# Down projection: more K tiles in seven-product form, one y buffer reloaded in halves, two operand sum buffers

## The chip, the cores and the metric

The kernel runs on one core of one Trainium2 chip. The metric is the device time of one execution in microseconds, given as the median of several runs. The profile is of one execution.

Names of the engines: PE is the tensor engine (PEld its weight loads), DVE the vector engine, ACT the scalar engine, POOL is GpSimd, and SP is the queue that issues the DMAs.

## The reference

One transformer block on x of 2048 tokens by 1024 columns, in bf16: a modulated layer norm, linear attention, a residual, a second modulated layer norm, and a gated feed-forward network with a residual. The part that matters here is the last line of the feed-forward network and its residual:

```python
def _B_ref(x, w_gate, w_up, w_down):              # D = 1024, F = 3584
    return _gelu(x @ w_gate) * (x @ w_up) @ w_down
...
h = _layernorm(x, axis=-1) * (1 + cb) + sb
x = x + gb * _B_ref(h, B_w_gate, B_w_up, B_w_down)
```

The product with `w_down` has 2048 rows, K = 3584 (28 K tiles of 128) and 1024 columns.

## The kernel before

Everything up to the feed-forward network stays as it is. The network runs in 28 units (`unit(u)`): two halves of the tokens, each with 14 units of 256 columns of F. Every unit leaves `y`, the gated product, for two K tiles of the down projection, and `y_store` writes it to a scratch tensor in DRAM (`scr_y`). `x1`, the input of the last residual, is also parked in DRAM (`scr_x`).

The down projection works on the 16 chunks of 128 tokens in eight pairs (ca, cb). A pair with the 1024 output columns in two halves is a 2 by 2 block product, once two K tiles (index r = 0, 1) are taken together: the left side has the blocks a0, a1 (chunk ca) and b0, b1 (chunk cb), the right side four blocks of w_down of 128 by 512. Instead of eight block products the kernel makes seven (Strassen-Winograd) for a number `nj(ca)` of such groups j, and the plain eight for the K tiles that are left (`down`, over `fcs`). The seven products are called P1 to P7. `d_prod(ca, b0, k)` issues Pk as `nj` matmuls of 128x128 by 128x512 into one of the four PSUM banks of the pair (b0 is 0 or 4).

- P1 and P2 take y and w_down as they are, in bf16.
- P5, P6, P7, P3 and P4 take sums of y blocks (`d_s(ca, i)`, i = 0 to 4, here called S0 to S4) and sums of w_down blocks (`d_t(i, q)`), both in the f32r type. S0 = b0 + b1, S1 = S0 - a0, S2 = a0 - b0, S3 = a1 - S1 are made on DVE, S4 is a copy of b1 made on ACT. P5 reads S0, P6 S1, P7 S2, P3 S3 and P4 S4. The sums of the weights are made once, for each part q of w_down (`WDT[q]`), and stay in SBUF.
- Between products, ACT and DVE copy or add PSUM banks (`dpcp`, `ducp`, `descp`, `dpadd`), so that each bank ends up with one quarter of the pair's output.
- `evac` then multiplies a quarter by the gate row (`x2a`), adds x1 (`x2b`) and stores it: two DVE instructions and one DMA.

Before the change `nj` is 6 for the first pair and 11 for the others; the sums have three buffers (`DS`); y of a pair has two alternating buffers `YA` for 22 K tiles and one buffer `YB` for the other 6; x1 comes in whole pairs into two buffers `XD`. The order of the products in a pair is P2 P6 P5 P7 P3 P4, and then the plain matmuls with P1 of the next pair among them (`d_first`). In the last pair plain matmuls are mixed in between, and P3 goes last, into a free bank, with the gate already multiplied into its weights (`t_gb`).

The order on each engine is the order in which these functions emit it; only the part before the second feed-forward unit is reordered by a planner (`sch.reorder`). Every buffer is a fixed stretch of one SBUF arena, and a tracker (`IntervalTracker`) adds the waits that follow from reads and writes of the same bytes or of the same PSUM bank. An engine, and SP too, takes its instructions strictly in order, so a DMA that waits holds up those emitted after it. Each SP DMA also waits for the DMA eight before it.

Of the kernel before, what the change touches and what calls it, by code (L numbers as in the profile page):

```python
# [65 lines left out]
NDJ = 11  # L66
NDJ0 = 6
NJQ = (2, 2, 2, 2, 2, 1)
WDQ = [OFF_R3, OFF_R3 + 8192, OFF_R3 + 16384, OFF_WS, OFF_HT + 16384, OFF_WS + 16384, OFF_WS + 8192, OFF_WS + 20480]
FCQ = [0, 4, 8, 12, 16, 20, 22, 26, NFC]  # L70
OFF_DT = (tuple(OFF_XALL + i * 4096 for i in range(4)), tuple(OFF_XALL + i * 4096 for i in range(4, 8)),
          (OFF_XALL + 32768, OFF_XALL + 36864, OFF_GUH, OFF_GUH + 4096),
          (OFF_TMP + 4096, OFF_TMP + 8192, OFF_R3 + 24576, OFF_YS[0]),
          (OFF_HT + 8192, OFF_HT + 12288, OFF_YS[1], OFF_YS[2]),
          (OFF_GAB, OFF_GAB + 2048, OFF_ROW, OFF_ROW + 2048))
OFF_DS = [OFF_YT + i * 5632 for i in range(3)]
OFF_XD = [OFF_HT + 24576, OFF_HT + 28672]
OFF_YA = [OFF_YT + 45056, OFF_YT + 16896]
OFF_YB = OFF_YT + 28160
# [250 lines left out]
def bass_adaLN_cond__linear_attn_block__geglu_ffn__prompt_kernel(  # L330
# [15 lines left out]
    scr_y = nc.dram_tensor("scr_y", [2 * CPG, P, NFC, 2 * P], bf16).ap()  # L346
    scr_x = nc.dram_tensor("scr_x", [P, NCH, D], bf16).ap()
    scr_rd = nc.dram_tensor("scr_rd", [NSG, 2, HPG, NG, SGW // 2], f32).ap()
    with ExitStack() as es:
# [31 lines left out]
        WDT = [at(f"wd{q}", [P, FCQ[q + 1] - FCQ[q], D], bf16, WDQ[q]) for q in range(8)]  # L381
        DT = [[at(f"dt{q}{i}", [P, NJQ[q], 512], f32r, o_) for i, o_ in enumerate(l)] for q, l in enumerate(OFF_DT)]
        DH = [at(f"dh{q}", [P, NJQ[q], 2, 512], f32r, WDQ[q]) for q in range(6)]
        DS = [at(f"ds{i}", [P, NDJ, P], f32r, OFF_DS[i]) for i in range(3)]
        DS0 = [at(f"dp{i}", [P, NDJ0, P], f32r, OFF_XD[i]) for i in range(2)]
# [962 lines left out]
        def wd_dma(q):  # L1348
            f0, f1 = FCQ[q], FCQ[q + 1]
            sch.dma(Q, lambda e: e.dma_start(WDT[q][:], wd_v[:, f0:f1, :]), wr=[t_ for fc in range(f0, f1) for t_ in r_wd(fc)], note=f"wd{q}")  # L1350
# [196 lines left out]
        def r_xd(c_, c0=0, c1=D):  # L1547
            i = c_ // 2 % 2
            o_ = OFF_XD[i] + c_ % 2 * 2048
            return [(o_ + c0 * 2, o_ + c1 * 2, f"xd{i}")]  # L1550

        def x_in(i):
            sch.dma(Q, lambda e: e.dma_start(XD[i % 2][:], scr_x[:, 2 * i:2 * i + 2, :]), wr=r_xd(2 * i) + r_xd(2 * i + 1), deps=[x_st[i // 2]], note=f"xd{i}")

        def y_in(i):
            sch.dma(Q, lambda e: e.dma_start(YA[i % 2][:], scr_y[i, :, 0:2 * NDJ, :]), wr=[(OFF_YA[i % 2], OFF_YA[i % 2] + NDJ * 1024, f"ya{i % 2}")],
                    deps=[y_st[u] for u in range(i // CPG * NFP, i // CPG * NFP + NDJ)], note=f"ya{i}")

        def yb_in(i):
            sch.dma(Q, lambda e: e.dma_start(YB[:], scr_y[i, :, 2 * NDJ:NFC, :]), wr=[(OFF_YB, OFF_YB + (NFC - 2 * NDJ) * 512, "yb")],  # L1560
                    deps=[y_st[u] for u in range(i // CPG * NFP + NDJ, (i // CPG + 1) * NFP)], note=f"yb{i}")

        def evac(c_, k, b, c0, c1):
            n = c1 - c0
            X_ = XD[c_ // 2 % 2][:, c_ % 2, c0:c1]
            sch.op(V, lambda e: e.tensor_tensor(PS(b, 0, n), PS(b, 0, n), GBB[:, c0:c1], ALU.mult), prd=pr(b), pwr=pr(b), rd=R_GBB, note=f"x2a c{c_}.{k}")
            sch.op(V, lambda e: e.tensor_tensor(X_, PS(b, 0, n), X_, ALU.add), prd=pr(b), rd=r_xd(c_, c0, c1), wr=r_xd(c_, c0, c1), note=f"x2b c{c_}.{k}")
            sch.dma(Q, lambda e: e.dma_start(out_v[:, c_, c0:c1], X_), rd=r_xd(c_, c0, c1), note=f"out{c_}.{k}")

        def r_y(c_, fc):  # L1570
            i, h = c_ // 2, c_ % 2
            o_, name = (OFF_YA[i % 2] + fc * 512, f"ya{i % 2}") if fc < 2 * NDJ else (OFF_YB + (fc - 2 * NDJ) * 512, "yb")
            return [(o_ + h * 256, o_ + h * 256 + 256, name)]

        def y_at(c_, fc):
            i, h = c_ // 2, c_ % 2
            return YA[i % 2][:, fc, h * P:(h + 1) * P] if fc < 2 * NDJ else YB[:, fc - 2 * NDJ, h * P:(h + 1) * P]

        def down(c_, k, b, c0, c1, fcs, last, after):
            n, o = c1 - c0, None  # L1580
            for fc in fcs:
                q, m = wq_of(fc)
                o = sch.op(T, lambda e, fc=fc, q=q, m=m: e.matmul(PS(b, 0, n), y_at(c_, fc), WDT[q][:, m, c0:c1], start=False, stop=last and fc == fcs[-1], skip_group_check=True),  # L1583
                           rd=r_y(c_, fc) + r_wd(fc), pwr=(pr(b) if after and fc == fcs[0] else ()), note=f"down c{c_} k{k} fc{fc}", overwrite_ok=after)
# [13 lines left out]
        def d_t(i, q):  # L1598
            j0, j1 = 0, NJQ[q]
# [11 lines left out]
            sch.op(V, lambda e: e.tensor_tensor(dst, in0, in1, ALU.subtract), rd=r0 + r1, wr=wr, note=f"{'dtsum' if j1 - j0 == 2 else 'dtone'} {q}.{i}")  # L1611

        DSB = (0, 1, 2, 0, 1)

        def nj(ca):
            return NDJ0 if ca == 0 else NDJ

        def ds_ap(ca, i, j0, j1):
            k = DSB[i]
            if ca == 0 and i < 2:  # L1620
                return DS0[k][:, j0:j1, :], [(OFF_XD[k] + j0 * 512, OFF_XD[k] + j1 * 512, f"dp{k}")]
            return DS[k][:, j0:j1, :], [(OFF_DS[k] + j0 * 512, OFF_DS[k] + j1 * 512, f"ds{k}")]

        def y_ap(c_, r, j0, j1):
            i, h = c_ // 2, c_ % 2
            return (YA[i % 2][:, 2 * j0 + r:2 * j1 - 1 + r:2, h * P:(h + 1) * P], [t_ for j in range(j0, j1) for t_ in r_y(c_, 2 * j + r)])

        def d_s(ca, i):
            cb, n = ca + 1, nj(ca)
            for j0, j1 in ((0, min(n, 6)), (6, n)):  # L1630
# [12 lines left out]
        def t_gb(q):  # L1643
            n = NJQ[q]
            t_, r_ = dt_ap(q, 3, 0, n)
            sch.op(V, lambda e: e.tensor_tensor(t_, t_.bitcast(f32), GBB[:, 512:1024].unsqueeze(1).to_broadcast([P, n, 512]), ALU.mult), rd=r_ + R_GBB, wr=r_,
                   note=f"{'dtsum' if n == 2 else 'dtone'} gb{q}")

        def d_prod(ca, b0, k, own=None):
            b = b0 + {1: 0, 2: 0, 5: 3, 6: 2, 7: 2, 4: 2, 3: 1}[k] if own is None else own  # L1650
            i = {1: None, 2: None, 5: 0, 6: 1, 7: 2, 3: 3, 4: 4}[k]
            o, n = None, nj(ca)
            for j in range(n):
# [5 lines left out]
                else:  # L1659
# [3 lines left out]
                    if i == 4:  # L1663
                        dst = dst.rearrange("p (h c) -> p h c", h=2)
                o = sch.op(T, lambda e, l_=l_, r_=r_, j=j, dst=dst: e.matmul(dst, l_[:, 0, :], r_, start=(k in (1, 5) or own is not None) and j == 0, stop=j == n - 1, skip_group_check=True),  # L1665
                           rd=rl + rr, pwr=(pr(b) if j == 0 else ()), note=f"down P{k} c{ca} j{j}", overwrite_ok=True)
# [4 lines left out]
        later = []  # L1671

        def evac_part(c_, k, b, c0, c1):
            X_ = XD[c_ // 2 % 2][:, c_ % 2, c0:c1]
            sch.op(V, lambda e: e.tensor_tensor(DE[:, :], PS(b), GBB[:, c0:c1], ALU.mult), prd=pr(b), rd=R_GBB, wr=R_DE, note=f"x2a c{c_}.{k}")
            sch.op(V, lambda e: e.tensor_tensor(DE[:, :], DE[:, :], X_, ALU.add), rd=r_xd(c_, c0, c1) + R_DE, wr=R_DE, note=f"x2b c{c_}.{k}")

        def evac_sum(c_, k, b, c0, c1):
            X_ = XD[c_ // 2 % 2][:, c_ % 2, c0:c1]
            sch.op(V, lambda e: e.tensor_tensor(X_, PS(b), DE[:, :], ALU.add), prd=pr(b), rd=R_DE, wr=r_xd(c_, c0, c1), note=f"x2b c{c_}.{k}")  # L1680
            sch.dma(Q, lambda e: e.dma_start(out_v[:, c_, c0:c1], X_), rd=r_xd(c_, c0, c1), note=f"out{c_}.{k}")

        def d_first(i):
            b0 = i % 2 * 4
            d_prod(2 * i, b0, 1)
            sch.op(A, lambda e: e.activation(PS(b0 + 2), PS(b0), ACTF.Copy), prd=pr(b0), pwr=pr(b0 + 2), note="dpcp")  # L1686

        def d_pair(i, hook):
# [3 lines left out]
            parts = tuple((ca + n // 2, n % 2, b0 + n, n % 2 * 512, n % 2 * 512 + 512) for n in range(4))  # L1692
            for k in (2, 6, 5, 7, 12, 4, 14, 15, 13, 3) if last else (2, 6, 5, 7, 3, 4):
                if k > 10:
                    x = parts[k - 12]
                    down(*x, fcs, True, True)
                    if k == 13:
                        evac_part(*x)
                    else:
                        evac(*x)  # L1700
                    continue
# [257 lines left out]
```

## Time and profile before

| | |
|---|---|
| median of 3 runs | 786.52 us (786.47 to 786.85) |
| the profiled execution | 786.35 us |
| its span | 784.6 us |
| PE busy | 774.4 us |
| DVE busy | 625.8 us |
| ACT busy | 375.0 us |
| DMA queue time, share of 16 engines | 59.6% |

The span runs from the first to the last instruction of the profiled execution. Matmuls are pipelined: their durations overlap, so a matmul's cost on PE is the spacing of two of them and not the duration in the list. The feed-forward units end at 602.2 us of the span and the down projection fills the rest. In the profile L1442 is a matmul of a feed-forward unit, L1665 one of the seven products, L1583 a plain one; L1641 and L1636 are the sums S0 to S3 and S4, L1566 and L1567 the two instructions of an eviction, L1556 and L1560 the loads of y.

### The profile page before, as it was taken

Reading aid. Unit: us, or ns where it says so; the run is one execution under the profiler, and the core shown is the slowest. Engines: PE = TensorE matmul, PEld = TensorE weight load, DVE = VectorE, ACT = ScalarE, POOL = GpSimd, SP = SyncE. Lnnn points to the kernel's source line nnn. Section 1 sums busy time; section 2 is a strip of 40 time slices with the busy share of each in tenths; the row PEclk is TensorE's granted clock in tenths of the full one; section 3 lists DMA queues with packets and bytes.
Section 4 is the critical chain, followed back from the end, with each engine's and each line's share of the span. In section 5 each row is a group of like instructions: output and inputs, shape, how many; then the busy total and the mean of one; then the engine's idle time right before and its main releaser. Section 6 shows DMA issues by size and latency. Waiting matters only on the chain.

```text
span 784.6 us, 10665 instructions
## 1 busy us (share of the span) xinstructions
PE 774.4 (99%) x3832; PEld 490.2 (62%) x3890; DVE 625.8 (80%) x949; ACT 375.0 (48%) x636; POOL 47.1 (6%) x126
## 2 busy tenths in 40 slices
PE   8999999999999999999999999999999999999998
PEld 4444445666445666767676776767676566666665
DVE  6699998895789878787989889898987975555586
ACT  2497743242565477877755555465654011111011
POOL 2131300000321011100000000000000000000000
PEclk9999999999999999999999999999999999999999
DMA  9789749939998257866344764534327644333411
GB/s 287 250 173 244 163 94 248 221 74 194 203 285 226 82 155 193 242 177 198 108 135 126 242 198 154 159 108 134 113 76 246 239 160 140 124 91 128 159 57 33
DMA packets 178781, 130.24 MB, mean 166 GB/s; under 512 B 69020, under 2 KB 163492, under 8 KB 176680
## 3 DMA queue, kind: packets, MB, share of 16 engines
q1 hardware_dynamic: 178712, 129.55, 59.6%
q8 instruction: 31, 0.51, 0.3%
q14 instruction: 22, 0.18, 0.1%
q10 hardware_dynamic: 16, 0.00, 0.0%
HBM read 92.55 MB, written 23.35 MB: 148 GB/s over the span
## 4 chain that ended last, share of the span: by engine, by line
PE 71%; DVE 1%; issue 0%; DVEq 0%
PE ps_all L1442 44%; PE ps_all L1665 17%; PE ps_all L1583 6%; PE ps_all L1268 4%; DVE h2a L726 0%; DVE xall L1276 0%; DVE xd L1680 0%; DVE ys L1472 0%; DVEq L1914 0%
## 5 line engine op out<-in xcount | busy, mean ns | idle before, releaser
L1442 PE MATMUL ps_all<-ss,tp 128*128 128x512 f32 x896 | 214.3, 396 | 0.0
L1442 PEld LDWEIGHTS ps_all<-ss,tp 128*128 128x128 f32 x896 | 168.2, 188 | 37.8 <-DVE ss L1397 0.3
L1465 ACT ACTIVATE ge<-ps_all 128x512 f32<-128x512 f32 x112 | 64.1, 597 | 74.3 <-DVE ps_all L1453 61.8
L1442 PE MATMUL ps_all<-h2a,wt 128*128 128x512 bf16 x421 | 95.6, 379 | 1.8
L1472 DVE TENSOR_TENSOR ys<-ge,ps_all 128x512 bf16<-128x512 f32 x112 | 74.4, 684 | 5.8 <-PE ps_all L1442 2.9
L1460 DVE TENSOR_TENSOR ps_all<-ps_all,es 128x512 f32<-128x512 f32 x54 | 37.7, 699 | 50.6 <-ACT es L1450 50.3
L1665 PE MATMUL ps_all<-dt,ds 128*128 128x512 f32 x320 | 76.2, 395 | 0.0
L1442 PEld LDWEIGHTS ps_all<-h2a,wt 128*128 128x128 bf16 x448 | 38.0, 98 | 57.2 <-ACT ps_all L1447 16.9
L1417 DVE TENSOR_TENSOR tp<-wt 128x1024 fp32r<-128x1024 bf16 x56 | 68.1, 1216 | 2.1 <-DMA wt<-in_B_w_up_dram 2.1
L1665 PEld LDWEIGHTS ps_all<-dt,ds 128*128 128x128 f32 x320 | 60.1, 188 | 13.4
L1417 DVE TENSOR_TENSOR tp<-wt,tp 128x1024 fp32r<-128x1024 bf16 x56 | 68.2, 1218 | 0.0
L933 PE MATMUL ps_all<-h1T,wq 128*128 128x512 bf16 x256 | 56.7, 379 | 0.0
L882 PE MATMUL ps_all<-wk,h1T 128*128 128x512 bf16 x239 | 55.3, 379 | 1.2 <-DMA wk<-in_A_wqkv_dram 0.5
L1268 PE MATMUL ps_all<-w,pq 128*128 128x512 bf16 x250 | 55.6, 379 | 0.4
L1442 PE MATMUL ps_all<-ar,tp 128*128 128x512 f32 x224 | 55.5, 390 | 0.0
L871 ACT ACTIVATE eb<-ps_all 128x512 f32<-128x512 f32 x64 | 36.4, 593 | 37.6 <-PE ps_all L882 14.8
L1442 PEld LDWEIGHTS ps_all<-ar,tp 128*128 128x128 f32 x224 | 42.0, 188 | 8.9
L1686 ACT ACTIVATE ps_all<-ps_all 128x512 f32<-128x512 f32 x8 | 4.7, 582 | 87.4 <-PE ps_all L1665 87.4
L1447 ACT ACTIVATE ps_all<-ps_all 128x512 f32<-128x512 f32 x56 | 32.6, 582 | 27.1 <-PE ps_all L1442 27.1
L933 PEld LDWEIGHTS ps_all<-h1T,wq 128*128 128x128 bf16 x256 | 24.9, 98 | 30.0
L1268 PEld LDWEIGHTS ps_all<-w,pq 128*128 128x128 bf16 x256 | 24.7, 98 | 30.0 <-ACT w L1200 0.3
L1583 PE MATMUL ps_all<-wd,yb 128*128 128x512 bf16 x185 | 42.6, 379 | 0.5
(148 smaller groups left out, 1016.0 us busy)
## 6 DMA issues: line engine op xcount, KB each, us to landing
wt<-in_B_w_gate_dram SPq DMA_DIRECT2D x28, 512.0 KB, 4.0
wt<-in_B_w_up_dram SPq DMA_DIRECT2D x28, 512.0 KB, 5.3
scr_y<-ys SPq DMA_DIRECT2D x28, 512.0 KB, 2.9
ya<-scr_y SPq DMA_DIRECT2D x8, 1408.0 KB, 6.6
rb<-scr_rd SPq DMA_DIRECT2D x32, 256.0 KB, 6.6
wmst<-in_w_mod_dram SPq DMA_DIRECT2D x6, 1024.0 KB, 5.7
wd<-in_B_w_down_dram SPq DMA_DIRECT2D x6, 1024.0 KB, 7.4
wmq<-in_w_mod_dram SPq DMA_DIRECT2D x8, 512.0 KB, 6.7
```

The source lines that it names most:

```text
L871: sch.op(A, lambda e: e.activation(EB[i][:, :], PS(bank), ACTF.Exp), prd=pr(bank), wr=rng, note=f"{note}.exp")
L882: o = sch.op(T, lambda e, dc=dc: e.matmul(PS(bank), H1[sg][:, ci, dc, :], W_[:, dc, jg * 512:(jg + 1) * 512], start=(dc == 0), stop=(dc == ...
L933: o = sch.op(T, lambda e, dc=dc: e.matmul(PS(b), WQ[:, dc, qc * P:(qc + 1) * P], H1[sg][:, :, dc, :], start=(dc == 0), stop=(dc == NDC - 1 ...
L1268: last[half] = sch.op(T, lambda e, g=g, half=half: e.matmul(PS(b0 + half), PQ[sg][:, g, ci * P:(ci + 1) * P], W2[:, g, half * 512:(half + ...
L1417: sch.op(V, lambda e: e.tensor_tensor(TP[k][:], in0, in1 if k in (0, 2) else in1[:], ALU.subtract), rd=r0 + r1, wr=r_tp(k), deps=[x1_ops[7 ...
L1442: o = sch.op(T, lambda e, l_=l_, r_=r_, dc=dc: e.matmul(PS(b), l_, r_, start=fresh and dc == 0, stop=dc == ND2 - 1, skip_group_check=True) ...
L1447: sch.op(A, lambda e: e.activation(PS(BB + t), PS(BA + t), ACTF.Copy), prd=pr(BA + t), pwr=pr(BB + t), note="pcp")
L1460: sch.op(V, lambda e: e.tensor_tensor(PS(BC + t), PS(BC + t), ES[t][:, :], ALU.add), prd=pr(BC + t), rd=r_2k(OFF_ES[t], f"es{t}"), pwr=pr( ...
L1465: sch.op(A, lambda e: e.activation(GE[i][:, :], PS(b), ACTF.Gelu_apprx_tanh), prd=pr(b), wr=r_2k(OFF_GE[i], f"ge{i}"), note="gelu")
L1472: sch.op(V, lambda e: e.tensor_tensor(YS[s_][:, 2 * h:2 * h + 2, t, :], q(GE[i][:, :]), q(PS(b + 1)), ALU.mult), rd=r_2k(OFF_GE[i], f"ge{i ...
L1583: o = sch.op(T, lambda e, fc=fc, q=q, m=m: e.matmul(PS(b, 0, n), y_at(c_, fc), WDT[q][:, m, c0:c1], start=False, stop=last and fc == fcs[- ...
L1665: o = sch.op(T, lambda e, l_=l_, r_=r_, j=j, dst=dst: e.matmul(dst, l_[:, 0, :], r_, start=(k in (1, 5) or own is not None) and j == 0, st ...
```

## The change

- `nj` becomes 6 for the first pair, 12 for the next two and 14, all 28 K tiles, for the last five.
- w_down is held in seven equal parts of four K tiles, and all seven get their sums. The sums of the last one lie where y of pair 1 was, and are made during pair 2 and the start of pair 3.
- y of a pair lies in two tiles, one for each r, 14 K tiles each. There is one such pair of tiles, `YA[0]`, for all pairs but pair 1, which has its own, `YA[1]`. From pair 2 on, the tile of r = 0 is loaded for the next pair as soon as S2 is made, that of r = 1 as soon as S4 is made (`y_next`). In pair 2, whose plain matmuls still read groups 12 and 13, those two groups are loaded after them (the loads noted `yt`).
- The scratch tensor of y is laid out by r, so that a store's pieces are 512 bytes instead of 1024.
- The operand sums have two buffers, each in two halves of seven groups; a pair uses them in turn.
- x1 comes in quarters (128 tokens by 512 columns) with one buffer each (`XQ`), instead of whole pairs with two.
- The order in a pair is P1 P5 P6 P2 P7 P3 P4, with the plain matmuls of one quarter after P2 and of the other three after P4 (pairs 1 and 2). In the last pair P3 is split: groups 6 to 13 go into its own bank before P4, groups 0 to 5 last.
- The evictions of pair 0 move into pair 1. The load of the fourth part of w_down is issued one unit earlier, and the y of pair 1 ahead of the last part of w_down.

The diff, cut to its core (in `ds_ap`, `k` and `h` are the buffer and its half):

```diff
-NDJ = 11
-NDJ0 = 6
-NJQ = (2, 2, 2, 2, 2, 1)
+NDJ = NFC // 2
+NJP = (6, 12, 12, NDJ, NDJ, NDJ, NDJ, NDJ)
+NSJ = NDJ // 2
...
-    scr_y = nc.dram_tensor("scr_y", [2 * CPG, P, NFC, 2 * P], bf16).ap()
+    scr_y = nc.dram_tensor("scr_y", [4 * CPG, P, NDJ, 2 * P], bf16).ap()
...
-        DS = [at(f"ds{i}", [P, NDJ, P], f32r, OFF_DS[i]) for i in range(3)]
-        XD = [at(f"xd{i}", [P, 2, D], bf16, OFF_XD[i]) for i in range(2)]
+        SB = [[at(f"sb{k}{h}", [P, NSJ, P], f32r, o_) for h, o_ in enumerate(l)] for k, l in enumerate(OFF_SB)]
+        XQ = [at(f"xq{n}", [P, 512], bf16, o_) for n, o_ in enumerate(OFF_XQ)]
...
-        YA = [at(f"ya{i}", [P, 2 * NDJ, 2 * P], bf16, OFF_YA[i]) for i in range(2)]
-        YB = at("yb", [P, NFC - 2 * NDJ, 2 * P], bf16, OFF_YB)
+        YA = [[at(f"ya{i}{r}", [P, NDJ, 2 * P], bf16, o_) for r, o_ in enumerate(l)] for i, l in enumerate(OFF_YA)]
...
+        def y_in(i, r, j0=0, j1=NDJ):
+            a = ya_of(i)
+            sch.dma(Q, lambda e: e.dma_start(YA[a][r][:, j0:j1, :], scr_y[2 * i + r, :, j0:j1, :]), ...)
...
         def ds_ap(ca, i, j0, j1):
-            k = DSB[i]
+            if ca == 0:
+                k, h = ((0, 0), (1, 0), (0, 1), (1, 1), (0, 0))[i]
+            else:
+                k, h = (ca // 2 + i) % 2, j0 // NSJ
...
         def d_pair(i, hook):
             ...
-            for k in (2, 6, 5, 7, 12, 4, 14, 15, 13, 3) if last else (2, 6, 5, 7, 3, 4):
+            def y_next(r):
+                if i > 1 and not last:
+                    y_in(i + 1, r, 0, nj(ca))
+
+            for k in (1, 5, 6, 2, 7, 3, 4):
                 if last and k == 3:
-                    d_prod(ca, b0, 3, 0)
-                    evac_sum(*parts[1][:2], 0, *parts[1][3:])
+                    d_prod(ca, b0, 3, None, range(6, NDJ))
+                    evac_part(*parts[1])
                     continue
                 d_prod(ca, b0, k)
+                if k == 1:
+                    d_cp(b0 + 2, b0, "dpcp")
                 elif k == 5:
+                    d_ecp(b0 + 3)
+                    d_s(ca, 2)
+                elif k == 6:
+                    d_add(b0 + 1, b0 + 2)
+                    d_s(ca, 3)
+                    y_next(0)
+                elif k == 2:
+                    fin(0)
                 elif k == 7:
+                    d_add(b0 + 3, b0 + 2)
+                    d_s(ca, 4)
+                    y_next(1)
+                    if not fcs:
+                        fin(3)
+                elif k == 3:
+                    if not fcs:
+                        fin(1)
+                    d_s(ca + 2, 0, (0, 1) if nj(ca) == nj(ca + 2) else (0,))
+                else:
+                    ns = (3, 1, 2) if fcs else (2,)
+                    for n in ns:
+                        std(n)
+                    if not last and nj(ca) != nj(ca + 2):
+                        for r in range(2):
+                            y_in(i + 1, r, nj(ca), NDJ)
+                    for n in ns[:-1]:
+                        evac(*parts[n])
+                    if not last and nj(ca) != nj(ca + 2):
+                        d_s(ca + 2, 0, (1,))
+                    evac(*parts[ns[-1]])
+                    if last:
+                        d_prod(ca, b0, 3, 0, range(6))
+                        evac_sum(*parts[1][:2], 0, *parts[1][3:])
+                    else:
+                        d_s(ca + 2, 1)
                 hook(k)
...
         DMAS = {...
-                14: lambda: wd_dma(0), 15: lambda: y_in(0), 16: lambda: wd_dma(1), 18: lambda: wd_dma(2)}
+                14: lambda: wd_dma(0), 15: lambda: (y_in(0, 0), y_in(0, 1)), 16: lambda: wd_dma(1), 18: lambda: wd_dma(2), 26: lambda: wd_dma(3)}
...
-        wd_dma(5)
-        wd_dma(7)
-        yb_in(0)
-        y_in(1)
+        y_in(1, 0)
+        y_in(1, 1)
+        wd_dma(6)
...
         def hooks(i):
             def hook(k):
...
+                if i == 1:
+                    if k == 1:
+                        y_in(2, 0)
+                        y_in(2, 1)
+                    if k in (1, 5):
+                        for n in (0, 1) if k == 1 else (2, 3):
+                            evac(*parts_of(0)[n])
+                    if k == 6:
+                        x_in(1, 0, 1, 2, 3)
+                else:
+                    if k == 1:
+                        x_in(i, 0, 3, 1)
+                    elif k == 5:
+                        x_in(i, 2)
+                    if i == 2 and k in (1, 2, 7, 3):
+                        d_t({1: 0, 2: 1, 7: 2, 3: 3}[k], 6)
+                    if i == 3 and k == 1:
+                        d_t(4, 6)
+                    if not more and k in (5, 6):
+                        for q in {5: (0, 1), 6: (2,)}[k]:
+                            t_gb(q)
```

`std(n)` issues the plain matmuls of quarter n, `fin(n)` those and then its `evac`.

More of the change, by code (lines that the diff above doesn't have):

```diff
@@ L511, in wq_of @@
         def wq_of(fc):
-            q = next(q for q in range(8) if fc < FCQ[q + 1])
-            return q, fc - FCQ[q]
+            return divmod(fc, 4)
         def r_wd(fc):
@@ L1559, in yb_in, with r_xq @@
-        def yb_in(i):
-            sch.dma(Q, lambda e: e.dma_start(YB[:], scr_y[i, :, 2 * NDJ:NFC, :]), wr=[(OFF_YB, OFF_YB + (NFC - 2 * NDJ) * 512, "yb")],
-                    deps=[y_st[u] for u in range(i // CPG * NFP + NDJ, (i // CPG + 1) * NFP)], note=f"yb{i}")
-        def evac(c_, k, b, c0, c1):
[L1564 to L1568, printed above, removed]
+        def r_xq(n):
+            return [(OFF_XQ[n], OFF_XQ[n] + 1024, f"xq{n}")]
@@ L1678, in evac_sum @@
         def evac_sum(c_, k, b, c0, c1):
[L1679 to L1686, printed above, removed]
+            n = 2 * (c_ % 2) + k
@@ L1691, in d_pair @@
             fcs = list(range(2 * nj(ca), NFC))
-            parts = tuple((ca + n // 2, n % 2, b0 + n, n % 2 * 512, n % 2 * 512 + 512) for n in range(4))
-            for k in (2, 6, 5, 7, 12, 4, 14, 15, 13, 3) if last else (2, 6, 5, 7, 3, 4):
[L1694 to L1701, printed above, removed]
+            parts = parts_of(i)
@@ L1719, in d_pair @@
-                if last and k in (6, 7):
-                    for q in range(3):
-                        t_gb(q if k == 6 else q + 3)
-                for x in mine:
-                    evac(*x)
-                if 0 < i and not last and k in (7, 3, 4):
-                    d_s(ca + 2, {7: 2, 3: 0, 4: 1}[k])
-                hook(k)
-                if i == 0 and k == 7:
-                    down(*parts[0], list(range(12, 16)), False, True)
-            assert not later
-            if last:
-                return
```

213 lines of the change are left out of this document (106 added, 107 removed).

## The prediction

> **What bounds the kernel now.** I read the page's parts 1, 2 and 4 first: which engine is busy, whether it is busy everywhere, and who is on the chain that ended last.
>
> ```profile
> span 784.6 us, 10665 instructions
> ...
> PE 774.4 (99%) x3832; PEld 490.2 (62%) x3890; DVE 625.8 (80%) x949; ACT 375.0 (48%) x636; POOL 47.1 (6%) x126
> ...
> PE   8999999999999999999999999999999999999998
> ...
> PEclk9999999999999999999999999999999999999999
> ...
> PE 71%; DVE 1%; issue 0%; DVEq 0%
> ```
>
> TensorE (PE) works without a break at the full granted clock, and the chain is made of its matmuls. So the time is the number of matmuls times their spacing, plus whatever makes PE wait. Next come the windows of one FFN unit and one down-projection pair, the chain inside that pair, and the list of waits from 590 us on.
>
> ```profile
> 475.26:487.82 12.56, 12.49 (x56) 8.86 (x56) 10.80 (x14) 6.73 (x13) 0.00 (x0) 1.00 0.67 209
> 641.47:663.93 22.46, 22.39 (x101) 14.75 (x101) 14.59 (x20) 3.12 (x5) 0.00 (x0) 1.00 0.54 186
> ```
>
> ```profile
> 641.47 0.07 issue
> 641.54 3.83 PE ps_all L1583 x17
> 645.37 2.37 PE ps_all L1665 x11
> 647.75 1.29 PE ps_all L1583 x6
> 649.04 14.89 PE ps_all L1665 x66
> 663.93 0.07 issue
> ```
>
> ```profile
> PEld ps_all L1583 <- issue: 2.6, 10, 0.3
> ...
> DVE ds L1641 <- DMA ya<-scr_y: 1.0, 1, 1.0
> ```
>
> A pair today is 101 matmuls in 22.46 us: 46 in bf16 (24 plain, 11 each of P1 and P2) and 55 in f32 (P5, P6, P7, P3, P4). No data holds PE up; its only gap is 0.07 us once per pair, where an f32 run ends and a bf16 run begins. An FFN unit is 16 bf16 and 40 f32 matmuls in 12.56 us. Two equations, 16b + 40f = 12.56 and 46b + 55f = 22.46, give b = 0.2163 us for a bf16 matmul and f = 0.2275 us for an f32 one, each stretch holding one such gap. This is the most important reading: the change swaps the cheap kind for the dear kind.
>
> **The change part by part. Matmuls.** With n groups of two K tiles in products, a pair costs 7n + 4(28 - 2n) = 112 - n matmuls. Pair 0 keeps n = 6. Pairs 1 and 2 go from 11 to 12, pairs 3 to 7 from 11 to 14: 2 + 15 = 17 groups more. One group replaces 8 plain bf16 matmuls by 2 bf16 and 5 f32: 6 x 0.2163 - 5 x 0.2275 = 0.160 us. Seventeen groups give **-2.73 us**. Counted by pair: pairs 1 and 2 become 40b + 60f = 22.30 us, pairs 3 to 7 become 28b + 70f = 21.98 us.
>
> The Trainium skill, page "TensorE: Matmul & The Clock Gate", section "Back-to-back issue gap", puts the isolated gap at N/2.4 + 2.5 ns, about 216 ns for 512 columns, with no difference between types; by it 17 matmuls fewer would be worth 3.7 us. The trace agrees for b and disagrees for f.
>
> **Order.** P1 P5 P6 P2 P7 P3 P4 instead of P2 P6 P5 P7 P3 P4 plain P1 has an f32 run end twice in pairs 1 to 6 (before: once) and once in the last (before: twice): five ends more at the 0.07 us gap shown, **+0.35 us**. Its bounds are 0 and 0.35: no run end is removed on balance, so a gain is excluded.
>
> **Operand sums and evictions.** These are the vector engine's (DVE) and scalar engine's (ACT) pieces:
>
> ```profile
> L1641 DVE TENSOR_TENSOR ds<-ya 128x768 fp32r<-128x768 bf16 x15 | 14.3, 951 | 1.0 <-DMA ya<-scr_y 1.0
> ...
> L1641 DVE TENSOR_TENSOR ds<-ya 128x640 fp32r<-128x640 bf16 x14 | 11.5, 818 | 0.0
> ...
> L1636 ACT ACTIVATE ds<-ya 128x768 fp32r<-128x768 bf16 x8 | 6.7, 839 | 0.0
> ...
> L1636 ACT ACTIVATE ds<-ya 128x640 fp32r<-128x640 bf16 x7 | 5.1, 728 | 0.0
> ```
>
> ```profile
> 659.59 3.29 DVE L1641 TENSOR_TENSOR ds<-ya 128x768 fp32r<-128x768 bf16 x4
> ...
> 666.69 0.69 DVE L1566 TENSOR_TENSOR ps_all<-ps_all,gbb 128x512 f32<-128x512 f32 x1
> 667.41 0.69 DVE L1567 TENSOR_TENSOR xd<-ps_all,xd 128x512 bf16<-128x512 f32 x1
> 668.02 0.69 DVE L1566 TENSOR_TENSOR ps_all<-ps_all,gbb 128x512 f32<-128x512 f32 x1
> ```
>
> A half of seven groups (896 elements) takes 951 + 133 = 1084 ns on DVE and 839 + 111 = 950 ns on ACT. Back to back the halves overlap a little (four took 3.29 us, not 3.54), so I space them by 1.0 us. One eviction (two instructions) is 1.33 us. DVE then has per pair 8 x 1.08 + 4 x 1.33 + 2 x 0.7 = 15.4 us in 22: not the bound. What counts is the order, since with two sum buffers each sum waits for the product that read its buffer: S2 for P5, S3 for P6, S4 for P7, the next S0 for P3, the next S1 for P4.
>
> **Reload of y.** The y buffer is single now, so the second half for the next pair is issued on SP only after S4 has read it. These are the transfers near in size, and the same load in the crowded stretch from 603 us:
>
> ```profile
> ya<-scr_y SPq DMA_DIRECT2D x7, 1408.0 KB, 6.6
> ...
> out_dram<-xd SPq DMA_DIRECT2D x32, 128.0 KB, 2.2
> yb<-scr_y SPq DMA_DIRECT2D x8, 384.0 KB, 3.5
> ```
>
> ```profile
> ya<-scr_y SPq DMA_DIRECT2D x1, 1408.0 KB, 10.1
> ```
>
> A line through 384 and 1408 KB gives 3.03 us per 1024 KB: 5.05 us for a half of 896 KB, 4.64 for 768 KB, 2.7 for 128 KB. Readers of a finished product start about 0.26 us after PE goes on: 0.17 us because a matmul lasts 395 ns at 228 spacing, and 0.09 us as at the end of the chain:
>
> ```profile
> L1665 PE MATMUL ps_all<-dt,ds 128*128 128x512 f32 x320 | 76.2, 395 | 0.0
> ```
>
> ```profile
> 779.00 2.52 PE ps_all L1665 x11
> 781.52 0.03 issue
> ...
> 781.61 0.69 DVE xd L1680
> ```
>
> Steady pair (3 to 7), from its first matmul: P1 ends at 3.03, P5 6.21, P6 9.40, P2 12.43, P7 15.61, P3 18.80, P4 22.05 us. S4's second half runs 15.87 to 16.82; SP issues the reload at 16.9; it lands at 21.95. S0 of the next pair is done in halves at 23.05 and 24.05, and P5 wants it at 25.08. DVE then evicts one quarter (25.4) and makes S1's first half (26.5); P6 wants it at 28.26. With 0.25 us for a weight load not yet in flight, 1.5 us are left. So the reload may take up to 6.6 us, which is just what the larger 1408 KB took: bounds 3.5 to 6.6, no stall at either end, **0**. Queued behind it on SP are only output stores and the x1 quarters, wanted 12 us later. The first half is issued after S2 (about 7.6 us) and lands by 13.
>
> Pair 2 to pair 3 differs: the plain matmuls at its end read groups 12 and 13, so these come as two 128 KB loads only when pair 2's last plain matmuls are done. From pair 2's start: P7 ends 14.25, the main second half is issued at 15.3 and lands at 19.95, S0's first half is done at 21.05, two evictions run to 23.6, plain ends at 22.30, the small loads are issued at 22.4 and 22.75. Pair 3's P1 wants group 12 at 24.97. With the 2.2 us of the 128 KB store they land at 24.6 and 24.95; S0's second half ends 26.1, an eviction comes before S1 on DVE, S1's first half ends 28.45, P6 wanted it at 28.58 less 0.25: stall 0.1. With 2.7 us from the line: 0.4 in P1, 0.2 in P6, together 0.6. With the 3.5 us of 384 KB: 1.4. Below, 0. I take **+0.4 us**, between the row of the same size and the line; S1 late again in pair 3 is absorbed by the 1.5 us.
>
> The skill's page "DMA: Bandwidth & Descriptors", section "Anatomy of one DMA", fits 2.0 us plus bytes at 436 GB/s, an estimate of 2.3 us for 128 KB, with which the stall would be about 0.2; its 5.3 us for 1408 KB is below the 6.6 measured.
>
> **Edits at nothing.** The stores of y go out in pieces of 512 instead of 1024 bytes. These rows bound them:
>
> ```profile
> wt<-in_B_w_gate_dram SPq DMA_DIRECT2D x28, 512.0 KB, 4.0
> ...
> scr_y<-ys SPq DMA_DIRECT2D x28, 512.0 KB, 2.9
> ```
>
> If a store takes the weights' 4.0 instead of 2.9 us, the three ys buffers and 12.56 us per unit hide it; without them it would cost 1.1 us a unit. One w_down load goes a unit earlier on SP; it waits for that unit's P2, and only a store a unit later stands behind it. In pair 0 the y of pair 1 is issued ahead of the last part of w_down; S0 of pair 1, which once waited 1.0 us for its y, has it earlier, and that part is wanted 17 us later. Pair 0's evictions and the last w_down sums move into DVE's idle time of pairs 1 to 3. At the end, P3's last 6 matmuls follow P4 instead of all 11; the eviction of P4's quarter (1.33 us) just fits under 6 x 0.2275 = 1.37: 0 to 0.1.
>
> Sum: -2.73 + 0.35 + 0.4 = -2.0 us. The profiled execution took 786.35 us (span 784.6 and 1.75 around it), so 784.35; the median of the runs, 786.52, lies 0.17 higher, so **784.5 us**, -0.25%. About 0.2% (1.57 us, a line at 784.95) is what a measurement of this kernel can tell from no change.
>
> **The rivals.** (a) *The y reload becomes the clock.* If a half takes longer than 6.6 us, P6 (then P5) waits at each of the four transitions 3 to 7; beyond 7.5 us the loss exceeds the gain and the 0.2% (4 x 0.9 = 3.6). With the 10.1 us of the crowded row: 4 x 3.5 = 14 us, 798.5. For: this is one serial loop S4, SP, load, S0, S1 where there were two buffers. Against: 10.1 was seen with other loads in the queue ahead of it; in the steady pairs only 128 KB stores run beside it. (b) *The two small loads take 3.5 us:* 1.4 us instead of 0.4, 785.5; against it stands the 2.2 us row of the same size, for it that this is a store and not a load. (c) *An f32 matmul costs no more than a bf16 one in longer runs:* 17 x 0.2163 = 3.68, net -2.9, 783.6. Against: 32 of an FFN unit's f32 matmuls stand in one run and the unit still averages 0.2243. The skill's gap rule above is this case. (d) *DVE order costs a little in every pair*, say 0.3 us in seven: 2.1 us, 786.6, no change; against: the 1.5 us left.
>
> **How the numbers follow.** Forecast 0.57 (784.0 to 785.3, three quarters of it below 784.95), a 0.20, b 0.12, c 0.04, d 0.07. Faster 0.43 + 0.04 = 0.47; same 0.14 + 0.12 + 0.07 = 0.33; slower 0.20. The range runs from c's end, 783.6, into the mild part of a, 788.5 (landing near 7.5 us), leaving out some 0.17.
>
> **What would show it.** Right: steady pairs of 98 matmuls in 22.0 to 22.1 us, pairs 1 and 2 of 100 in about 22.35, PE without waits except up to 1 us around the start of pair 3 (for a small load, then for S1), and halves landing in 4.5 to 6 us. Wrong: PE waiting for DVE's sums at the start of P5 or P6 in every pair (a), waits of over 1 us for the small loads (b), pairs of 21.2 us (c), or short waits spread over all pairs (d).

## The result, and the profile after

The changed kernel takes 784.49 us (median of 8 runs, 783.81 to 785.08) against 786.68 for the kernel before, run beside it (median of 8): 2.19 us less, ratio 0.9971 (95% interval 0.9960 to 0.9982). The forecast was 784.5 us, 0.25% faster. From here on the times of the experiments stand beside these 784.49 us; each experiment also has its own runs of the kernel before.

First the page of the changed kernel: the span, PE's busy time, PE in 40 slices, and the chain.

```profile
span 782.7 us, 10766 instructions
...
PE 776.1 (99%) x3873; PEld 495.4 (63%) x3873; DVE 638.4 (82%) x950; ACT 375.5 (48%) x630; POOL 46.6 (6%) x126
...
PE   8999999999999999999999999999999999999998
...
PE 93%; SPq 2%; DVE 2%; DMA 2%; issue 1%; ACT 0%; DVEq 0%; ACTq 0%
```

PE is still the bound from end to end. Every matmul has one weight load, and the weight loads are 17 fewer than before (3873 against 3890), as the code has it; before's 3832 matmuls are no count, because some matmul records are missing from that trace.

The windows of pairs 1, 3, 4 and 5, each from the start of its P1 to the next pair's (columns: us, then busy us and count by engine):

```profile
624.59:646.90 22.31, 22.31 (x101) 15.01 (x100) 15.30 (x22) 2.87 (x4) 0.00 (x0) 1.00 0.41 136
...
669.21:691.40 22.19, 22.19 (x100) 15.64 (x98) 17.21 (x23) 3.08 (x4) 0.00 (x0) 1.00 0.48 153
691.40:713.44 22.04, 22.04 (x100) 15.73 (x99) 15.07 (x19) 3.09 (x4) 0.00 (x0) 1.00 0.42 132
```

```profile
713.44:735.48 22.04, 22.04 (x100) 15.73 (x99) 15.05 (x19) 3.09 (x4) 0.00 (x0) 1.00 0.40 132
```

A pair took 22.46 us before. Pairs of 12 groups take 22.31, pairs of 14 take 22.04, and pair 3 takes 0.15 more. The list of waits from 590 us on has just one wait of PE for a sum, and DVE's own wait for y is longer than it was (10.2 us against 1.0):

```profile
DVE sb L1638 <- DMA ya<-scr_y: 10.2, 6, 4.6
...
PEld ps_all L1662 <- DVE sb L1638: 0.3, 1, 0.3
```

The timeline around that wait, at the start of pair 3. The two small loads of groups 12 and 13 are issued at 669.19, S0's second half can start at 671.93, an eviction follows it, S1 starts at 674.35, and the weight load of P6 stands 0.32 us for it.

```profile
669.19 0.79 SPq L1557 DMA_DIRECT2D ya<-scr_y  x2
...
671.93 1.09 DVE L1638 TENSOR_TENSOR sb<-ya,ya 128x896 fp32r<-128x896 bf16 x1 [0.29 <-DMA ya<-scr_y]
...
672.94 0.69 DVE L1562 TENSOR_TENSOR ps_all<-ps_all,gbb 128x512 f32<-128x512 f32 x1
673.74 0.69 DVE L1563 TENSOR_TENSOR xq<-ps_all,xq 128x512 bf16<-128x512 f32 x1
674.35 2.08 DVE L1638 TENSOR_TENSOR sb<-sb,ya 128x896 fp32r<-128x896 f32 x2
...
675.48 3.04 PEld L1662 LDWEIGHTS ps_all<-dt,sb 128*128 128x128 f32 x14 [0.32 <-DVE sb L1638]
```

The DMAs from 600 us on (size of one, median us to landing):

```profile
ya<-scr_y SPq DMA_DIRECT2D x12, 896.0 KB, 4.9
...
ya<-scr_y SPq DMA_DIRECT2D x2, 768.0 KB, 5.4
...
ya<-scr_y SPq DMA_DIRECT2D x2, 128.0 KB, 2.0
```

And the end, where the last six matmuls of P3 follow P4:

```profile
778.20 1.52 PE L1662 MATMUL ps_all<-dt,sb 128*128 128x512 f32 x6
778.40 0.70 DVE L1562 TENSOR_TENSOR ps_all<-ps_all,gbb 128x512 f32<-128x512 f32 x1 [1.37 <-PE ps_all L1662]
779.20 0.69 DVE L1563 TENSOR_TENSOR xq<-ps_all,xq 128x512 bf16<-128x512 f32 x1
779.81 0.68 DVE L1675 TENSOR_TENSOR xq<-ps_all,de 128x512 bf16<-128x512 f32 x1
```

The last eviction starts at 779.81, 0.09 us after the matmuls end (778.20 + 1.52 = 779.72), the same distance as before: the eviction of P4's quarter just fits.

Where the time came from: the down projection starts with P2 of pair 0, at 602.06 us in the profiled execution before and at 602.56 here (the first row is of the kernel before, the second of the changed one).

```profile
602.06 1.47 PE L1665 MATMUL ps_all<-wd,ya 128*128 128x512 bf16 x6
```

```profile
602.56 1.47 PE L1662 MATMUL ps_all<-wd,ya 128*128 128x512 bf16 x6
```

From there to the span's end it takes 182.54 us before and 180.14 here: 2.40 us less. The 0.5 us lost ahead of it was lost in the attention part and the first feed-forward unit, whose code is the same. The first feed-forward matmuls come 0.28 us later and those after the first pause 0.57 us later, all before the first store of y; the rows before and after:

```profile
241.85 3.62 PE L1442 MATMUL ps_all<-h2a,wt 128*128 128x512 bf16 x15
...
252.38 2.11 PE L1442 MATMUL ps_all<-ss,tp 128*128 128x512 f32 x8
```

```profile
242.13 3.62 PE L1440 MATMUL ps_all<-h2a,wt 128*128 128x512 bf16 x16
...
252.95 2.14 PE L1440 MATMUL ps_all<-ss,tp 128*128 128x512 f32 x8
```

From the second of these rows to P2 of pair 0 it is 349.7 us before and 349.6 us here, so the feed-forward network after it is as fast as it was.

### The profile page after: what moved, and what is told of

It is laid out like the page before. It is cut to its first block, busy times and chain, and to the rows that moved or that the text cites. A ratio compares the mean times of both kernels' runs of the same rounds, so it can differ in the third digit from the quotient of the medians.

```text
span 782.7 us, 10766 instructions
## 1 busy us (share of the span) xinstructions
PE 776.1 (99%) x3873; PEld 495.4 (63%) x3873; DVE 638.4 (82%) x950; ACT 375.5 (48%) x630; POOL 46.6 (6%) x126
## 4 chain that ended last, share of the span: by engine, by line
PE 93%; SPq 2%; DVE 2%; DMA 2%; issue 1%; ACT 0%; DVEq 0%; ACTq 0%
PE ps_all L1440 44%; PE ps_all L1662 20%; PE ps_all L895 7%; PE ps_all L931 7%; PE ps_all L1266 6%; PE ps_all L880 5%; PE ps_all L1580 3%; DMA wmq<-in_w_mod_dram 1%; SPq L598 1%; SPq L603 1%; DVE ss L1395 1%; DMA h1T<-xh 0%; PE ps_all L913 0%; PE ps_all L1196 0%; DVE pq L1256 0%
## 5 line engine op out<-in xcount | busy, mean ns | idle before, releaser
L1440 PE MATMUL ps_all<-h2a,wt 128*128 128x512 bf16 x448 | 101.6, 380 | 0.0
L1662 PE MATMUL ps_all<-dt,sb 128*128 128x512 f32 x400 | 97.2, 398 | 0.0
L1662 PEld LDWEIGHTS ps_all<-dt,sb 128*128 128x128 f32 x400 | 75.1, 188 | 17.5 <-DVE sb L1638 0.3
L880 PE MATMUL ps_all<-wk,h1T 128*128 128x512 bf16 x248 | 56.9, 379 | 0.7 <-DVE h1T L724 0.6
L1662 PE MATMUL ps_all<-wd,ya 128*128 128x512 bf16 x200 | 45.9, 380 | 0.0
L1445 ACT ACTIVATE ps_all<-ps_all 128x512 f32<-128x512 f32 x56 | 32.6, 582 | 26.9 <-PE ps_all L1440 26.9
L880 PEld LDWEIGHTS ps_all<-wk,h1T 128*128 128x128 bf16 x248 | 23.6, 98 | 29.4 <-DVE h1T L724 3.0
```

Of the source, the lines that this page charges most:

```text
L880: o = sch.op(T, lambda e, dc=dc: e.matmul(PS(bank), H1[sg][:, ci, dc, :], W_[:, dc, jg * 512:(jg + 1) * 512], start=(dc == 0), stop=(dc == ...
L1440: o = sch.op(T, lambda e, l_=l_, r_=r_, dc=dc: e.matmul(PS(b), l_, r_, start=fresh and dc == 0, stop=dc == ND2 - 1, skip_group_check=True) ...
L1445: sch.op(A, lambda e: e.activation(PS(BB + t), PS(BA + t), ACTF.Copy), prd=pr(BA + t), pwr=pr(BB + t), note="pcp")
```

## The experiments

**Twelve groups in all pairs** (`nj12`). It tells the price of a group from the prices of order and buffers. With 12 groups every pair has plain matmuls again, pairs 2 to 6 end with the small loads, and S1 of the next pair is made ahead of the evictions.

```diff
-NJP = (6, 12, 12, NDJ, NDJ, NDJ, NDJ, NDJ)
+NJP = (6, 12, 12, 12, 12, 12, 12, 12)
...
-                    if i == 2 and k in (1, 2, 7, 3):
-                        d_t({1: 0, 2: 1, 7: 2, 3: 3}[k], 6)
...
```

> Groups in products: 12 in all of pairs 1 to 7 (10 fewer than in the changed kernel, 7 more than before), same order of products, same buffers; the weight sums of the last four K tiles are not made, S1 of the next pair is made ahead of the evictions, and the output is the same function. Theory A (the prediction's prices, 0.160 us a group from b = 0.2163 and f = 0.2275, each end of an f32 run 0.07): 10 x 0.160 = 1.6 us slower than the changed kernel, a steady pair of 100 matmuls at 22.44. Theory B (the two pair lengths in the trace of the changed kernel, 22.31 for 40 bf16 + 60 f32 and 22.04 for 28 + 70, with run ends free: b = 0.2137, f = 0.2294, 0.135 a group): 1.35 us slower, pairs at 22.31. Rival (an f32 matmul costs as much as a bf16 one): 10 x 0.216 = 2.2 us slower, pairs at 21.6.

Measured: 785.99 us (median of 11), 1.5 us slower than the changed kernel; against the kernel before 0.9996 (0.9987 to 1.0005), no difference that can be told. A steady pair, in its window:

```profile
691.37:713.68 22.31, 22.20 (x99) 15.02 (x100) 13.84 (x19) 2.87 (x4) 0.00 (x0) 1.00 0.39 129
```

22.31 us in pairs 1 to 6, where A said 22.44 and B 22.31. B had its prices from pairs of 12 groups of this very order, so that it is met here does not yet speak for it. Two groups more make 22.04, so a group is worth 0.135 us in this order. The cheap f32 matmul (pairs at 21.6) is out. It also shows that the change lives on the pairs of 14: with 12 it would gain next to nothing.

**Sums in bf16** (`bf16sums`). All products have bf16 operands; buffers, orders and counts stay, and DVE makes the sums faster (the last rows of this document).

```diff
-        DT = [[at(f"dt{q}{i}", [P, 2, 512], f32r, o_) ...
-        SB = [[at(f"sb{k}{h}", [P, NSJ, P], f32r, o_) ...
+        DT = [[at(f"dt{q}{i}", [P, 2, 1024], bf16, o_) ...      # used: [:, :, 0:512]
+        SB = [[at(f"sb{k}{h}", [P, NSJ, 2 * P], bf16, o_) ...   # used: [:, :, 0:P]
```

> The changed kernel with the sums of y and of w_down kept in bf16 instead of f32r, so the precision of the five products changes; all buffers, orders and counts stay. It turns 500 f32 matmuls into bf16 ones. Theory A: 500 x (0.2275 - 0.2163) = 5.6 us and some 13 run ends at 0.07 = 0.9, together 6.5 us faster, a steady pair 98 x 0.2163 = 21.2 us. Theory B (run ends free, f - b = 0.0157): 7.9 us faster, a steady pair 98 x 0.2137 = 20.9 us. Rival (the type does not matter, what a pair costs beyond 98 x 0.2157 is waiting on operands): no change, pairs stay at 22.04.

Measured: 777.74 us, 6.75 us faster than the changed kernel (ratio to before 0.9884, 0.9871 to 0.9898). A steady pair:

```profile
709.32:730.47 21.15, 21.05 (x97) 9.60 (x98) 11.41 (x18) 3.08 (x4) 0.00 (x0) 1.00 0.40 137
```

21.15 / 98 = 0.2158 us for a bf16 matmul. Theory A holds (0.2163, 6.5 us) and B, which got its two prices from two pairs 0.27 us apart, falls (7.9 us). With b = 0.2158, an f32 matmul comes to 0.2279 in the pairs of before and to 0.2280 in those of 12 groups ((22.46 - 46 x 0.2158) / 55 and (22.31 - 40 x 0.2158) / 60) and to 0.2285 in those of 14, run ends included. What a pair takes beyond 98 bf16 matmuls is the type, not waiting: in the steady pairs of the changed kernel PE waits for no sum, so DVE's faster sums have nothing to save there.

**P2 in two parts** (`p2split`): one more end of an f32 run in each pair.

```diff
-                d_prod(ca, b0, k)
+                half = nj(ca) // 2
+                d_prod(ca, b0, k, None, range(half) if k == 2 else None)
...
                 elif k == 7:
+                    d_prod(ca, b0, 2, None, range(half, nj(ca)))
...
```

The plain matmuls and the eviction of quarter 0 move behind the second part.

> The changed kernel with the second half of P2 moved behind P7 in pairs 1 to 7, so that each pair has one more end of an f32 run; counts and sums stay, and no operand is late by the trace. Theory A (an end costs the 0.07 us gap shown at it): 7 x 0.07 = 0.5 us slower, a steady pair 22.11. Theory B (the gap at the end of an f32 run is given back at the start of the next one; a pair costs 28b + 70f whatever the order): 0, pairs stay at 22.04. A third possibility, a switch that costs the 0.26 us for which the weight load stood: 7 x 0.26 = 1.8 us slower.

Measured: 784.97 us (median of 10), 0.5 us slower; the intervals against the kernel before overlap, so what follows is read from the trace. Two steady pairs in one window, and the place in pair 1 where P7 waits:

```profile
714.04:758.19 44.15, 43.94 (x195) 31.30 (x197) 30.00 (x37) 6.17 (x8) 0.00 (x0) 1.00 0.39 132
```

```profile
633.52 0.69 DVE L1685 TENSOR_TENSOR ps_all<-ps_all,de 128x512 f32<-128x512 f32 x1
...
634.26 2.63 PEld L1662 LDWEIGHTS ps_all<-dt,sb 128*128 128x128 f32 x12 [0.79 <-DVE ps_all L1685]
```

A pair is 44.15 / 2 = 22.075 us: one end costs 0.035 us, between A (0.07) and B (0). The larger loss is one that the expectation had denied: in pair 1 DVE is evicting pair 0, so the addition that frees P7's bank comes late, and the pair takes 22.96 us instead of 22.31.

**The reload later by one small load** (`reload_late`).

```diff
                 if i > 1 and not last:
+                    if i > 2 and r == 1:
+                        y_in(i + 1, r, 0, 1)
                     y_in(i + 1, r, 0, nj(ca))
...
```

> The changed kernel, but for the four transitions 3 to 7 the second half of y waits for a first small load (64 KB, the first group of the same half) to land, about 2.1 us later than now. My theory (a serial loop S4, SP, load, S0, eviction, S1 with 1.5 us left by the prediction, 1.4 by the trace of the changed kernel): PE waits 0.6 to 0.7 us for S1 at P6 in each of four transitions, 2.4 to 2.8 us slower. Rival 1 (the load has more cover, since P5 could start late without harm): nothing. Rival 2 (each delay is paid in full): 4 x 2.1 = 8.4 us slower.

Measured: 784.85 us, no difference to speak of, but the edit did not do what it was for. The small load and the whole half in the timeline:

```profile
685.10 2.09 SPq L1557 DMA_DIRECT2D ya<-scr_y  x2
...
691.93 2.09 DVE L1638 TENSOR_TENSOR sb<-ya,ya 128x896 fp32r<-128x896 bf16 x2 [1.67 <-DMA ya<-scr_y]
```

The load of the first group needs only S4's first half to be done, so it went out at 685.10, ahead of S4's second half, and held the whole half up by some 0.2 us only: S0 started 0.37 us later than in the changed kernel (691.93, with pair 3 starting 0.22 us later, against 691.34). It tells nothing on the loop's slack.

**The reload later, mended** (`reload_wait`): the load ahead brings the last group, which S4 reads last.

```diff
-                        y_in(i + 1, r, 0, 1)
+                        y_in(i + 1, r, NDJ - 1, NDJ)
```

> As the kernel whose reload waited for the first group, but the small load ahead (64 KB) now brings the last group of the same half, which S4 reads last; so it cannot be issued before S4 is done, and the whole half follows only when it has landed: some 1.8 to 2.1 us later than in the changed kernel, in the four transitions 3 to 7. My theory (serial loop S4, SP, load, S0, eviction, S1; the trace of the changed kernel leaves about 1.35 us at P6): PE waits 0.45 to 0.75 us for S1 in each, 1.8 to 3 us slower than the changed kernel, a steady pair 22.5 to 22.8. Rival 1 (more cover than the sum shows): nothing, pairs at 22.04. Rival 2 (the delay is paid in full): 8 us, pairs at 24.

Measured: 784.60 us (median of 10). Two steady pairs, and PE's waits in the stage:

```profile
713.27:735.50 22.23, 22.12 (x98) 15.59 (x99) 14.96 (x18) 3.09 (x4) 0.00 (x0) 1.00 0.42 135
735.50:757.93 22.43, 22.32 (x97) 15.56 (x99) 14.96 (x18) 3.09 (x4) 0.00 (x0) 1.00 0.39 131
```

```profile
PEld ps_all L1662 <- DVE sb L1638: 2.3, 7, 0.7
```

The wait of PE for S1 appears, and it is the mechanism that was named, but smaller than expected: 0.2 and 0.4 us in these pairs, and the stage as a whole is 1.1 us longer in the profile (159.2 us from the start of pair 1 to the end of the span, against 158.1) where 1.8 to 3 was expected. Of the 1.1 us only 0.7 lies in the four transitions that the edit delays; 0.4 lies in pair 3, whose start it leaves as it was. The medians differ by 0.1 us, which can't tell this from nothing, so the price is read from one trace. The rows of the first transition tell how much was left: S0 starts 1.61 us after P1's weight loads begin, where it began 0.05 us ahead of them in the changed kernel (691.34 and 691.39); with 1.66 us of delay P6's weight load stands 0.16 us for S1. The two pairs above agree: there S0 starts 1.74 and 1.92 us after the pair does (the last two rows), and 0.19 and 0.39 us are lost. So 1.5 us were free, as the prediction had it, and not the 1.35 of the expectation.

```profile
691.19 2.71 PEld L1662 LDWEIGHTS ps_all<-wd,ya 128*128 128x128 bf16 x14 [0.26 <-issue]
...
692.80 2.09 DVE L1638 TENSOR_TENSOR sb<-ya,ya 128x896 fp32r<-128x896 bf16 x2 [3.08 <-DMA ya<-scr_y]
...
697.35 3.05 PEld L1662 LDWEIGHTS ps_all<-dt,sb 128*128 128x128 f32 x14 [0.16 <-DVE sb L1638]
...
715.01 2.09 DVE L1638 TENSOR_TENSOR sb<-ya,ya 128x896 fp32r<-128x896 bf16 x2 [3.23 <-DMA ya<-scr_y]
...
737.42 2.09 DVE L1638 TENSOR_TENSOR sb<-ya,ya 128x896 fp32r<-128x896 bf16 x2 [3.40 <-DMA ya<-scr_y]
```

**The second half loaded twice** (`reload_twice`): as above with `y_in(i + 1, r, 0, NDJ)` ahead.

> The changed kernel with the second half of y loaded twice, one after the other, in the four transitions 3 to 7: it is there some 5 us later. My theory: 5.0 less 1.35 us left, 3.6 us in each of four transitions, 14.6 us slower, 799; a steady pair 25.7. This is the prediction's rival a with its price. Rival: with the sums behind DVE's own queue the loss is larger, 5 us in each, 20 us.

Measured: 799.53 us, 15.0 us slower than the changed kernel, ratio to before 1.017 (1.0154 to 1.0185). Two pairs, and the wait of P5 for S0 in the one before them:

```profile
716.20:742.47 26.27, 23.81 (x98) 16.80 (x99) 14.96 (x18) 3.09 (x4) 0.00 (x0) 0.94 0.45 145
742.47:767.59 25.12, 22.41 (x98) 15.57 (x99) 14.96 (x18) 3.09 (x4) 0.00 (x0) 1.00 0.45 152
```

```profile
695.69 2.09 DVE L1638 TENSOR_TENSOR sb<-ya,ya 128x896 fp32r<-128x896 bf16 x2 [6.15 <-DMA ya<-scr_y]
...
696.84 3.04 PEld L1662 LDWEIGHTS ps_all<-dt,sb 128*128 128x128 f32 x14 [3.12 <-DVE sb L1638]
```

The loop is right: this is rival a of the prediction, made to happen. That its price came out near the 14.6 us expected is in part luck. The four delayed pairs are 3.1, 4.2, 3.1 and 4.2 us longer in the trace, together 14.6, but the granted clock (the share of its full speed that PE was given) was 0.94 in the second and the last of them and 1.00 in the others. So the waiting is about 3.1 us a pair, 12.4 in all, where 3.6 a pair was expected, and about 2.2 us are clock. Why the clock fell in two of the four is not shown.

**The store layout of before** (`store1k`): pieces of 1024 bytes out, 512 in.

```diff
-scr_y[2 * i + r, :, j0:j1, :]
+scr_y[i, :, 2 * j0 + r:2 * j1 - 1 + r:2, :]
...
```

> The changed kernel with the scratch tensor of y laid out as before: stores in pieces of 1024 bytes again, loads of y in pieces of 512 instead of 7168. My theory: the stores were hidden and stay so; a 896 KB load in 512-byte pieces takes 5.5 to 6 us (512 KB of weights in such pieces took 4.0) instead of 5.0, still within the loop's 6.3: no difference, pairs at 22.04. Rival 1 (the small pieces make the load longer than 6.3 us): PE waits for S1 in every transition, pairs over 22.2, 1 us slower or more. Rival 2 (the 512-byte stores cost something in the feed-forward units): 0.5 us faster, down stage starting earlier.

Measured: 784.37 us (median of 7), no difference. The loads from 672 us on:

```profile
ya<-scr_y SPq DMA_DIRECT2D x8, 896.0 KB, 5.8
```

5.8 us instead of 4.9, and the steady pairs stay at 22.04 us. The feed-forward units take as long as with the other layout (349.7 us from the first pause to P2 of pair 0), so the stores were hidden: the layout alone is worth nothing that these runs can tell.

**S1 ahead of the eviction** (`s1_first`), in pair 3 alone.

```diff
                         d_s(ca + 2, 0, (1,))
+                        d_s(ca + 2, 1)
                     evac(*parts[ns[-1]])
...
```

> The changed kernel with S1 of pair 3 made ahead of the last eviction of pair 2 on DVE; a look at the profile only. My theory (the one wait of PE in the stage is P6 of pair 3 for S1, which stands behind S0's late half and an eviction): that wait goes, pair 3 takes 22.04 instead of 22.19 us, the rest stays. Rival (PE waits for the small load itself): pair 3 stays at 22.19.

Measured: 784.39 us in a single run; pair 3 in its window:

```profile
669.31:691.31 22.00, 21.93 (x98) 15.71 (x98) 17.07 (x22) 3.08 (x4) 0.00 (x0) 1.00 0.46 155
```

The 0.15 us of pair 3 are gone and PE no longer waits for a sum in the stage. The wait was for S1, which stood behind S0's late half and an eviction; PE never waited for a small load itself.

**The feed-forward sums in bf16 too** (`bf16all`): the same edit as in `bf16sums` on the activation sums `SS`, the weight sums `TP` and the copy `A22R` of the feed-forward units.

> The kernel with the down sums in bf16, and the feed-forward units' sums of activations and weights in bf16 too, so the precision of their five products changes as well; counts, buffers and orders stay. If the surcharge belongs to the f32 type wherever it stands (12.56 us for 16 bf16 and 40 f32 matmuls, 0.2158 for a bf16 one as the pairs of bf16 sums show): each of 28 units takes 56 x 0.2158 = 12.08 us, 28 x 0.48 = 13.3 us faster than with down sums alone in bf16, about 764.4. Rival (the units are paced by something else, ACT's copies or DVE's sums): units stay over 12.3 us and less than half of that comes.

Measured: 764.41 us, ratio to before 0.9718 (0.9701 to 0.9734), the fastest version here. Two units in the timeline of PE:

```profile
333.53 3.62 PE L1440 MATMUL ps_all<-h2a,wt 128*128 128x512 bf16 x16
...
345.61 3.62 PE L1440 MATMUL ps_all<-h2a,wt 128*128 128x512 bf16 x16
```

A unit takes 12.08 us instead of 12.56, as expected. This version and `bf16sums` beat both kernels, at the price of precision named in their expectations; how much precision that is was not measured here.

## Why the prediction was right

**The matmuls: right in kind, the size uncertain.** The term was -2.73 us with b = 0.2163 and f = 0.2275. The bf16 sums give b = 0.2158 directly and f = 0.2279 to 0.2285 with the run ends in it. The prices were right to 0.5%, but the term is a difference of two large numbers: a group from 12 to 14 came to 0.135 us, not 0.160.

**The ends of f32 runs: half the size.** 0.07 each was taken from the gap that the chain shows; `p2split` gives 0.035. The first weight load after an f32 run stands 0.26 us, but the end costs 0.035, so most of that stand is not paid for.

By pairs, the errors of the two terms nearly cancel, and that is luck: 22.37 us was forecast for 12 groups (22.31 measured) and 22.05 for 14 (22.04).

**The reload loop: right, with its margin.** S0 of the next pair was forecast to start 21.95 us after a pair began; in the profile it starts at 713.36 for the pair that began at 691.40, 21.96 us.

```profile
713.36 2.09 DVE L1638 TENSOR_TENSOR sb<-ya,ya 128x896 fp32r<-128x896 bf16 x2 [1.41 <-DMA ya<-scr_y]
```

The halves landed in 4.9 us (5.05 forecast; the line through the two rows rises by 3.1 us per 1024 KB, not 3.03, and it is 3.1 that gives the 5.05). `reload_twice` shows that the loop bites when the load is late, at somewhat less than the price forecast once the clock is taken out; `reload_wait` shows that it starts to bite at 1.5 us.

**The small loads: mechanism right, size in the range of the runs.** They landed in 2.0 us (2.2 to 2.7 taken), P1 did not wait, and the wait at P6 made pair 3 0.15 us longer than a steady pair, where 0.4 was taken for the whole. With 2.2 us the working gave 0.1; the choice between the row of the same size and the line was the loose part. But 0.15 is the figure of one execution: with the code of this transition unchanged, pair 3 was 0.3 us longer than a steady pair in `reload_late` and `reload_twice` and 0.55 in `reload_wait`. The prediction also quotes a fit from the Trainium skill, page "DMA: Bandwidth & Descriptors", section "Anatomy of one DMA". The section gives that fit for DMAs issued by GpSimd; the loads here are issued by SP, so it is no price for them.

**Edits at nothing: right.** The stores (3.2 us instead of 2.9 to landing), the end, the earlier load of w_down and pair 0's evictions made no wait; `store1k` undoes the first without a difference. That pair 0's evictions move into pair 1 is not right, though: before the change, too, they were issued in pair 1, one behind each of P2, P6, P5 and P7 (in the trace from 625.36 to 638.71 us). Now two stand behind P1 and two behind P5.

The sum for the stage was -2.0 us and came out as -2.40: 0.25 us of the difference are the small loads, the rest is mostly pairs 1 and 2, at 22.31 instead of 22.37. The part ahead of the stage was 0.5 us slower in this profiled execution. That need not be an effect of the change: over the eight experiments other than `bf16all`, all of which contain it, the same row, P2 of pair 0, starts anywhere from 601.76 us (`store1k`) to 602.79 (`reload_late`), and before's 602.06 lies among them. In these eight traces and the two shown above, the stretch from the row after the first pause to this one takes 349.6 to 349.7 us, so the whole spread comes from ahead of 254 us, before any y is stored. What moves it is not settled. So it is luck too that the median lies 0.01 us from the forecast: the stage gained 0.4 us more than forecast, and in the profiled execution the part ahead of it gave 0.5 back.

```profile
601.76 1.47 PE L1662 MATMUL ps_all<-wd,ya 128*128 128x512 bf16 x6
```

```profile
602.79 1.47 PE L1662 MATMUL ps_all<-wd,ya 128*128 128x512 bf16 x6
```

Of the rivals, b, c and d did not occur, and a is the one to which the kernel is closest.

## What to carry to other kernels

When an engine is full, price a trade of many cheap operations for fewer dear ones by the spacing of each kind, solved from two stretches with different mixes, and not by their number: 17 matmuls fewer, in the new order, were worth 2.4 us by the lengths of the pairs (2 x 0.15 and 5 x 0.42), not 3.7. Before giving up a double buffer, write out the loop release, issue, landing, preparation, use against the clock of the engine that must not wait: here it closed with 1.5 us to spare, and loading a half twice cost 15 us, some 2 of them by a lower clock. And when the dear kind is dear only by its type, ask first whether the type is needed: on this kernel bf16 sums everywhere were worth nine times the change (20.1 us against 2.2), if the precision allows them.

## What the runs showed of the hardware that was not expected

An f32r matmul of 128x128 by 128x512 costs 0.012 us (5.6%) more than a bf16 one: 40 of them are the 0.48 us between units of 12.56 and 12.08 us, and in the pairs of 14 groups, where f32 runs are up to 42 long, the surcharge is no smaller (0.2285 against 0.2158). Its weight load takes longer (188 ns against 98), though less than the spacing; what makes the surcharge is not shown. With bf16 operands the steady pairs run at 0.2158 us a matmul and the units at 0.2157. The weight loads in the changed kernel and in `bf16sums`:

```profile
L1662 PEld LDWEIGHTS ps_all<-dt,sb 128*128 128x128 f32 x400 | 75.1, 188 | 17.5 <-DVE sb L1638 0.3
```

```profile
L1662 PEld LDWEIGHTS ps_all<-dt,sb 128*128 128x128 bf16 x194 | 19.0, 98 | 22.9
```

DVE also gains by the type: the sums of 896 elements took 621 ns with bf16 results and 1088 with f32r ones, from the same inputs:

```profile
L1638 DVE TENSOR_TENSOR sb<-ya,ya 128x896 fp32r<-128x896 bf16 x12 | 12.7, 1088 | 11.1 <-DMA ya<-scr_y 10.2 <-PE ps_all L1662 1.0
```

```profile
L1638 DVE TENSOR_TENSOR sb<-ya,ya 128x896 bf16<-128x896 bf16 x6 | 3.5, 621 | 4.3 <-DMA ya<-scr_y 4.3
```
